# Alternating the taps of two gate groups and moving reciprocals apart on VectorE in a sparse-attention and gated-projection kernel

## The chip, the cores and the metric

The kernel runs on one core of a Trainium2 chip. The core has TensorE (PE in the profile, with its weight loads listed as PEld), VectorE (DVE), ScalarE (ACT), GpSimd (POOL) and a queue that only issues transfers (SP). The metric is the device time of one execution in microseconds; lower is better. The time of the kernel before is the median of three runs.

## The reference

The inputs are q, k and v of 4 batches, 8 heads, 768 positions and 64 dimensions, a table of 3 sampled key blocks for each of 24 blocks of 32 positions, and the weights of a gated projection. All are float32.

```python
scores = q @ k.T / sqrt(64)                      # per batch and head
mask = |blk_i - blk_j| <= 1 or blk_i in (0, 23) or blk_j in (0, 23) or blk_j in sampled_blocks[blk_i]
attn = softmax(where(mask, scores, -1e9))        # the sum gets 1e-9 added before the division
x = (attn @ v), heads side by side               # [4, 768, 512]
gate_pre[t] = sum over k in 0..4 of conv_w[k] * xp[t + k]      # xp: x with 4 zero rows ahead
out = (sigmoid(gate_pre) * (x @ w_val)) @ w_out
```

So each output row needs the attention of its block of queries, a causal convolution of five taps along the sequence for the gate, and two dense 512x512 products.

## The kernel before, in words

**Units and steps.** Query blocks are worked in pairs. A batch has 11 ordinary pairs (each query block sees 8 key blocks) and one global pair (blocks 0 and 23, which see all 24) that is cut into two units. That makes 48 pairs and 52 units. The main loop (line 762) runs one step per unit, and in step n TensorE gets, in this order: the scores of unit n (tiles `sc`, or `s` for a global unit), the weighted values of unit n-2 (`av`), the transposes that bring the finished pair of unit n-3 into channel order (`xp`), the transposes of the weights of unit n-1 (`pt`), and then pieces of the projection (`vp` for x @ w_val, `op` for the product with w_out). The digits of `FILLS` say how many of those pieces a half step gets.

**Order on the engines.** Every engine executes its instructions in the order in which the Python code emits them (`InOrder`, line 77). An instruction that waits holds up all that stand behind it on the same engine.

**A unit on the other engines.** VectorE takes the row maxima of the scores (`mx`, line 457); ScalarE takes the exponentials (`pe`), and after the transposes it copies `pt` to `ptr` (line 475), which the `av` products use as weights. The column of ones in v makes the denominators part of `av`. At the end of a pair `values` (line 479) has VectorE add 1e-9 to the denominators (`rs<-av`), take the reciprocal (`rs<-rs`), and multiply (`x<-av,rs`). There is one `av` buffer (pool `ps_av`, bufs=1), so the next pair's `av` products can't start until `x` has read it. `x` is needed again by the `xp` transposes one step later. All 512 channels sit in four groups of 128 (`CH`), 384 positions at a time, which gives 8 tiles of rows.

**The gate.** `gates` (line 559) is a generator that works one tile of 384 rows. Its accumulators are four slices of `th`. For group f, ScalarE writes tap 0 (`first`, tile form `th<-xT,cw`), VectorE adds taps 1 to 4 (`th<-xT,cw,th`), each on top of the one before, and ScalarE applies a tanh (`th<-th`). The call of `first` for a group and the tanh of a finished one are put behind certain taps. `prepare` (line 721) advances the generators: the digits of `STEPS` say how many times per half step. It first decodes the weights, which arrive as 64-bit numbers, on VectorE and ScalarE (`words`, `wst`, `wv`, `wo`), and only then the gate. After those, it advances `split` (line 589: `xh` on ScalarE and `xl` on VectorE, the two halves of x that `vp` multiplies). `behind` (line 179) delays a call to the start of the next half step while `holding[0]` is set.

Of the kernel before, what the change touches and what calls it, by code (L numbers as in the profile page):

```python
# [12 lines left out]
ALU = mybir.AluOpType  # L13
# [3 lines left out]
B, H, S, D = 4, 8, 768, 64  # L17
# [5 lines left out]
CH = 4  # L23
# [41 lines left out]
def attention_moe(ctx, tc, qb, kb, v, ve, sampled, w_val, conv_w, w_out, ident_in, slot_in, out):  # L65
# [29 lines left out]
    pe, dve, act, pool, sp = (InOrder(e) for e in (nc.tensor, nc.vector, nc.scalar, nc.gpsimd, nc.sync))  # L95
# [83 lines left out]
    def behind(*calls):  # L179

        if holding[0]:
            waiting.extend(calls)
        else:
            for call in calls:
                call()

    def run(calls):
        while calls:
            calls.pop(0)()
# [97 lines left out]
    for bt in batches:  # L287
        order = list(range(NP - 1))
        order.insert(GLOB_AT[bt.b], -1)
        for place, p in enumerate(order):  # L290
            pr = Pair()
# [187 lines left out]
    def values(un):  # L479
        pr = un.pr  # L480
        if un.e == 0:
            pr.av = ps_av.tile([128, 2, 2, DV], F32, tag="av", name="av")
        if pr.glob:
            for h in range(2):
                for c in range(6):
                    pt = un.PT[4 * h + c if c < 4 else 4 + 2 * h + c]
                    for hp in range(HP):
                        cols = slice(BLK * hp, BLK * hp + BLK)
                        hd = 2 * hp + h
                        matmul(  # L490
                            pr.av[cols, un.e, h, :], pt[:, cols], pr.bt.vn[:, c, hd * DV : (hd + 1) * DV],
                            start=c == 0, stop=c == 5, tile_position=(0, BLK * hp),
                        )
        else:
            slots = [(a, h, b, (4 * a + 2 * b + h) * DV) for a in range(2) for h in range(2) for b in range(2)]
            wide = pr.bt.b < WIDE
            if wide:
                for a, h, b, hd in slots:
                    matmul(
                        pr.av[64 * b : 64 * b + 64, a, h, :], un.PT[4 * h + 2 * a][:, 64 * b : 64 * b + 64],  # L500
                        pr.va[:, hd : hd + DV], start=a + h == 0, stop=False, tile_position=(0, 64 * b),
                    )
            for a, h, b, hd in slots:
                for c in range(1 if wide else 0, 2):
                    for j in range(2):
                        rows = slice(64 * b + BLK * j, 64 * b + BLK * j + BLK)
                        vt = pr.vb[:, j, :] if c else pr.va
                        matmul(
                            pr.av[rows, a, h, :], un.PT[4 * h + 2 * a + c][:, rows], vt[:, hd : hd + DV],
                            start=c == 0, stop=a + h == 2 if wide else c == 1, tile_position=(0, rows.start),  # L510
                        )
        if un.last:
            rs = three.tile([128, 2, 2, 2], F32, tag="rs", name="rs")
            dve.tensor_scalar_add(rs[:, 0], pr.av[:, :, :, D], 1e-9)
            dve.reciprocal(rs[:, 1], rs[:, 0])
            pr.x = two.tile([128, 2, 2, D], F32, tag="x", name="x")
            dve.tensor_tensor(
                out=pr.x, in0=pr.av[:, :, :, 0:D], in1=rs[:, 1, :, :, None].to_broadcast([128, 2, 2, D]), op=ALU.mult
            )

    def finish(pr):
# [37 lines left out]
    def gates(m):  # L559

        xT, t, n = m.bt.xT, m.t, m.n
        m.th = two.tile([128, CH, TS], F32, tag="th", name="th")
        acc = [m.th[:, f, 0:n] for f in range(CH)]

        def first(f):
            act.activation(acc[f], xT[:, f, t : t + n], AF.Copy, scale=cw[:, f, 0:1])

        def tanh(f):
            act.activation(acc[f], acc[f], AF.Tanh, scale=0.5)

        first(0)
        yield
        for f in range(CH):
            for k in range(1, KW):
                dve.scalar_tensor_tensor(
                    out=acc[f], in0=xT[:, f, t + k : t + k + n], scalar=cw[:, f, k : k + 1], in1=acc[f],
                    op0=ALU.mult, op1=ALU.add,
                )
                if k == 1 and f + 1 < CH:
                    behind(lambda f=f: first(f + 1))  # L580
                if f and k == 2:
                    behind(lambda f=f: tanh(f - 1))
                yield
        yield
        tanh(CH - 1)
        m.bt.read.add(("gate", m.t))
        yield
# [17 lines left out]
                m.bt.read.add(("split", m.t))  # L605
            yield

    late = []

    def project(m):  # L610

# [76 lines left out]
    def advance(jobs, after=None):  # L688

        m, g = jobs[0]  # L690
        try:
            next(g)
        except StopIteration:
            jobs.pop(0)
            if after is not None:
                after(m)
# [18 lines left out]
    def fill(times=1):  # L715
        for _ in range(times):
            if may_project():
                run(late)
                advance(to_project)

    def prepare(steps):
        for k in range(steps):
            if k == 1:
                run(late)
            if next(decoding, None):
                continue

            if to_gate and (to_gate[0][0].begun or len(gating) < 2):
                to_gate[0][0].begun = True
                gating.add(id(to_gate[0][0]))  # L730
                advance(to_gate, prepared)
        run(late)

        if {CH, CH + 1} <= decoded and len(staged) == 2 * CH and to_split and unread <= {id(to_split[0][0])}:
            advance(to_split, prepared)


    at = {"keys": 0, "values": 0, "copied": 0, "scaled": 0}
# [23 lines left out]
    for n in range(N + LAG_V):  # L762
        step[0] = n

        def more_keys():
            return more("keys", freed(n - 1) + RING, load_keys)

        def more_values():
            return more("values", freed(n - LAG_V - 1) + VRING, load_values)

        if n == 0:
            more_keys()
            numbers_first = {eng: list(block_numbers(pairs[0], eng)) for eng in (POOL, ACT)}
            until("scaled", 0, scale)
            indices(0)
            until("copied", 0, copy_keys)
            more_keys()
            until("copied", 1, copy_keys)
            more_values()
        else:  # L780
            while more_keys() or more_values():
                more_values()
        until("scaled", n + (SCALE_AHEAD if n else 1), scale)
        store()
        k = len(staged)
        if k < 2 * CH and n >= WEIGHTS_AT[k] and (k < 4 or k - 4 in decoded):
            next(weights)

        second_half = []
        if n < N:  # L790
            second_half.append(scores(units[n]))
            if not (n and units[n - LAG_T].pr.glob and units[n - LAG_T].pr.bt.b < HI_MOE):
                run(second_half)
        if n == 0:
            more_keys()
        until("copied", n + COPY_AHEAD, copy_keys)
        if n == 0:
            while more_keys() or more_values():
                more_values()
        if 0 <= n - LAG_V < N:  # L800
            values(units[n - LAG_V])
        if n >= LAG_V:
            while more("values", freed(n - LAG_V) + VRING, load_values):
                pass
        ending = [finish(units[n - LAG_X].pr)] if n >= LAG_X and units[n - LAG_X].last else []
        full = n < N and units[n].pr.glob and units[n].pr.bt.b >= HI_MOE
        for end in ending:
            if not full:
                next(end)

        def end_pairs():
            while ending:
                for _ in ending.pop(0):
                    pass

        if 0 <= n - LAG_T < N:
            pieces = 3 if units[n - LAG_T].pr.glob else 2
            for half, _ in enumerate(transposes(units[n - LAG_T])):
                at_half = 2 * n + min(half, 1)
                run(second_half)  # L820
                run(waiting)
                if half + 1 == pieces:
                    run(copies)
                    end_pairs()
                fill(int(FILLS[at_half]))
                holding[0] = half + 1 < pieces and not may_project()
                prepare(int(STEPS[at_half]))
                holding[0] = False
        else:
            fill(1)  # L830
            prepare(int(STEPS[2 * n]))
        if n == N + LAG_V - 1:
            ending.append(finish(units[N - 1].pr))
        end_pairs()
# [53 lines left out]
```

## Time and profile before

| | |
|---|---|
| Device time, median of 3 runs | 373.05 us (371.3, 373.05, 377.46) |
| Span of the profiled execution | 372.1 us |
| TensorE busy | 349.9 us, 94% of the span |
| VectorE busy | 270.6 us, 73% |
| ScalarE busy | 254.3 us, 68% |
| GpSimd busy | 144.9 us, 39% |
| Taps `th<-xT,cw,th` on VectorE | 128 instructions, 79.2 us |
| `x<-av,rs`, reciprocal, denominators on VectorE | 48 each: 20.4, 8.6 and 7.4 us |

The profiled execution's own time outside the profiler isn't given; its span lies 0.95 us below the median and within the three times. A span is counted from the first to the last instruction. In the rows below a time in front is the start from the beginning of the span, and the second number is a length. A row with xN stands for N instructions that follow one another, and its length runs from the first start to the last end, so that two rows of one engine may overlap by a few hundredths.

### The profile page before, as it was taken

The page shows a single profiled execution, that of the slowest core. Times are in us where ns is not written, and L with a number is a line of the kernel's source. Part 1 is how long each engine was busy: PE and PEld are TensorE (multiplying, and loading weights), DVE is VectorE, ACT ScalarE, POOL GpSimd, SP SyncE. Part 2 cuts the span into 40 slices and gives each one's busy share as a digit, 9 for nine tenths or more (in the row PEclk, how much of TensorE's full clock was granted, in tenths as well). Part 3 has the DMA queues.
Part 4 walks back from the last instruction along what each step waited for, and adds up shares of the span by engine and source line. Part 5 has one row for each costly group of instructions (what it writes and reads, how often), then busy time and mean ns, then how long its engine had stood idle before and what let it go on. Part 6 is the DMA issues. An engine that isn't in the chain of part 4 may idle for free.

```text
span 372.1 us, 15481 instructions
## 1 busy us (share of the span) xinstructions
PE 349.9 (94%) x6274; PEld 276.1 (74%) x6274; DVE 270.6 (73%) x618; ACT 254.3 (68%) x619; POOL 144.9 (39%) x237
## 2 busy tenths in 40 slices
PE   8689998888998999999999999999999999999995
PEld 7456665556666787788779877787888779889894
DVE  4246789888978888678978867577669865979540
ACT  2568689899787857758687587666658766764421
POOL 1856683866573333633352063522531143000000
PEclk9959999999999999999999999999999999999999
DMA  7978886889987365798879367898664373110102
GB/s 229 278 241 277 283 281 226 237 219 299 286 257 248 109 167 146 188 315 232 262 203 289 107 173 214 218 288 250 192 195 130 98 232 99 55 58 28 75 11 85
DMA packets 52582, 72.35 MB, mean 194 GB/s; under 512 B 6944, under 2 KB 34720, under 8 KB 52512
## 3 DMA queue, kind: packets, MB, share of 16 engines
q1 hardware_dynamic: 44896, 47.69, 42.0%
q0 software_dynamic: 7040, 23.43, 22.1%
q8 instruction: 50, 0.82, 0.9%
q10 hardware_dynamic: 576, 0.24, 0.2%
q14 instruction: 20, 0.16, 0.2%
HBM read 65.05 MB, written 6.29 MB: 192 GB/s over the span
## 4 chain that ended last, share of the span: by engine, by line
PE 78%; DVE 8%; ACT 7%; issue 4%; another core or an unknown queue 1%; DMA 1%; ACTq 0%; DVEq 0%
PE vp L83 18%; PE op L83 18%; PE av L83 15%; PE pt L83 11%; PE sc L83 10%; PE xp L83 4%; PE s L83 3%; DVE mx L83 2%; ACT pe L83 2%; ACT ptr L83 2%; DMA sb<-in_sampled 1%; DVE xl L83 1%; DVE wst L83 1%; ACT first L83 1%
## 5 line engine op out<-in xcount | busy, mean ns | idle before, releaser
L83 POOL DMA_INDIRECT vb<-in_v,idx x88 | 87.4, 993 | 158.9 <-PE av L83 129.9
L83 ACT ACTIVATE pe<-sc,mx 128x256 f32<-128x256 f32 x176 | 69.6, 476 | 50.2 <-DVE mx L83 46.3
L83 DVE SCALAR_TENSOR_TENSOR th<-xT,cw,th 128x384 f32<-128x384 f32 x128 | 79.2, 626 | 7.5 <-ACT th L83 5.5
L83 DVE TENSOR_REDUCE mx<-sc 128x2 f32<-128x512 f32 x88 | 56.8, 684 | 38.1 <-PE sc L83 24.6
L83 ACT COPY ptr<-pt 128x512 f32<-128x512 f32 x112 | 64.4, 603 | 9.6 <-PE pt L83 7.1
L83 PE MATMUL sc<-kg,qc 64*32 64x256 f32 x1408 | 54.6, 388 | 6.9 <-DVE cst L83 3.4
L83 POOL COPY kg<-k 128x256 f32<-128x256 f32 (+1 forms) x143 | 56.8, 434 | 9.1 <-DMA k<-in_k 8.0
L83 PE MATMUL op<-wo,yh 128*128 128x512 f32 x192 | 53.6, 401 | 0.0
L83 PE MATMUL vp<-xh,wv 128*128 128x384 f32 x256 | 51.3, 341 | 0.0
L83 PE MATMUL pt<-ident,pe 128*128 128x128 f32 x352 | 50.9, 280 | 0.0
L83 PEld LDWEIGHTS av<-va,ptr 128*32 128x32 f32 (+1 forms) x1056 | 32.2, 119 | 24.9 <-issue 16.4
L83 PE MATMUL av<-va,ptr 128*32 128x65 f32 (+1 forms) x1056 | 42.7, 228 | 4.0 <-issue 3.1
L83 PEld LDWEIGHTS pt<-ident,pe 128*128 128x128 f32 x352 | 42.0, 144 | 3.3 <-DMA qc<-in_q 0.4
L83 PEld LDWEIGHTS vp<-xh,wv 128*128 128x128 f32 x256 | 44.2, 188 | 0.2
L83 PEld LDWEIGHTS sc<-kg,qc 64*32 64x32 f32 x1408 | 24.1, 107 | 26.9 <-issue 16.9
L83 PEld LDWEIGHTS op<-wo,yh 128*128 128x128 f32 x192 | 34.7, 188 | 6.6
L83 PE MATMUL av<-vb,ptr 128*32 128x65 f32 x1408 | 38.3, 224 | 1.3 <-issue 1.3
L83 PEld LDWEIGHTS av<-vb,ptr 128*32 128x32 f32 x1408 | 30.3, 111 | 3.3 <-issue 1.8
L83 PE MATMUL op<-wo,yl 128*128 128x512 f32 x96 | 31.6, 410 | 0.0
L83 ACT CAST yh<-y 128x384 fp32r<-128x384 f32 x32 | 16.6, 519 | 20.4 <-DVE y L83 19.8
L83 DVE SCALAR_TENSOR_TENSOR y<-th,vp 128x384 f32<-128x384 f32 x32 | 17.6, 549 | 13.7 <-PE vp L83 12.3
L83 PE MATMUL vp<-xl,wv 128*128 128x384 f32 x128 | 27.3, 335 | 0.0
(72 smaller groups left out, 441.1 us busy)
## 6 DMA issues: line engine op xcount, KB each, us to landing
kg<-in_k SPq DMA_DIRECT2D x165, 64.0 KB
vn<-in_v SPq DMA_DIRECT2D x12, 520.0 KB
qc<-in_q SPq DMA_DIRECT2D x48, 128.0 KB
k<-in_k SPq DMA_DIRECT2D x12, 512.0 KB
out<-ot SPq DMA_DIRECT2D x23, 256.0 KB
va<-in_v SPq DMA_DIRECT2D x44, 130.0 KB
wst<-in_w_val SPq DMA_DIRECT2D x4, 512.0 KB
wst<-in_w_out SPq DMA_DIRECT2D x4, 512.0 KB
```

The costliest lines, as they stand in the source:

```text
L83: made = getattr(self.eng, name)(*args, **kwargs)
```

## The change

Three things are edited. In `values`, the reciprocal and the product of a finished pair are no longer emitted at once: they go into a list `drip`. A new function `drop` emits from that list, one entry after each advance in `prepare`, one after a step's last transposes, and what is left at the end of the step. In `gates`, `first` is called for two groups at the start and the taps of two groups alternate; the calls of `first` for the other two groups and of the tanhs move accordingly.

```diff
         if un.last:
             rs = three.tile([128, 2, 2, 2], F32, tag="rs", name="rs")
             dve.tensor_scalar_add(rs[:, 0], pr.av[:, :, :, D], 1e-9)
-            dve.reciprocal(rs[:, 1], rs[:, 0])
+            drip.append(lambda: dve.reciprocal(rs[:, 1], rs[:, 0]))
             pr.x = two.tile([128, 2, 2, D], F32, tag="x", name="x")
-            dve.tensor_tensor(
-                out=pr.x, in0=pr.av[:, :, :, 0:D], in1=rs[:, 1, :, :, None].to_broadcast([128, 2, 2, D]), op=ALU.mult
+            drip.append(
+                lambda: dve.tensor_tensor(
+                    out=pr.x, in0=pr.av[:, :, :, 0:D], in1=rs[:, 1, :, :, None].to_broadcast([128, 2, 2, D]), op=ALU.mult
+                )
             )
...
         first(0)
+        first(1)
         yield
-        for f in range(CH):
+        for g in range(0, CH, 2):
             for k in range(1, KW):
-                dve.scalar_tensor_tensor(
-                    out=acc[f], in0=xT[:, f, t + k : t + k + n], scalar=cw[:, f, k : k + 1], in1=acc[f],
-                    op0=ALU.mult, op1=ALU.add,
-                )
-                if k == 1 and f + 1 < CH:
-                    behind(lambda f=f: first(f + 1))
-                if f and k == 2:
-                    behind(lambda f=f: tanh(f - 1))
-                yield
+                for f in (g, g + 1):
+                    dve.scalar_tensor_tensor(
+                        out=acc[f], in0=xT[:, f, t + k : t + k + n], scalar=cw[:, f, k : k + 1], in1=acc[f],
+                        op0=ALU.mult, op1=ALU.add,
+                    )
+                    if g == 0 and k < 3 and f == 1:
+                        behind(lambda k=k: first(k + 1))
+                    if g and k == 1:
+                        behind(lambda f=f: tanh(f - 2))
+                    yield
+        behind(lambda: tanh(CH - 2))
         yield
         tanh(CH - 1)
...
+    def drop(times=2):
+        while drip and times:
+            drip.pop(0)()
+            times -= 1
+
     def prepare(steps):
         for k in range(steps):
             if k == 1:
                 run(late)
             if next(decoding, None):
+                drop(1)
                 continue
 
             if to_gate and (to_gate[0][0].begun or len(gating) < 2):
                 to_gate[0][0].begun = True
                 gating.add(id(to_gate[0][0]))
                 advance(to_gate, prepared)
+                drop(1)
         run(late)
...
                 if half + 1 == pieces:
                     run(copies)
                     end_pairs()
+                    drop(1)
                 fill(int(FILLS[at_half]))
...
+        drop()
         if n == N + LAG_V - 1:
```

What this does to the order of instructions is shown at three places. The first is VectorE at the last pair before the dense products start (122 us in the trace). Before:

```order
L83 TENSOR_REDUCE mx<-sc 128x2 x2
L83 TENSOR_SCALAR rs<-av 128x4
L83 RECIPROCAL rs<-rs 128x4
L83 TENSOR_TENSOR x<-av,rs 128x256
L83 SCALAR_TENSOR_TENSOR th<-xT,cw,th 128x384 x3
```

The same place now:

```order
L83 TENSOR_SCALAR rs<-av 128x4
L83 SCALAR_TENSOR_TENSOR th<-xT,cw,th 128x384
L83 RECIPROCAL rs<-rs 128x4
L83 SCALAR_TENSOR_TENSOR th<-xT,cw,th 128x384
L83 TENSOR_TENSOR x<-av,rs 128x256
L83 SCALAR_TENSOR_TENSOR th<-xT,cw,th 128x384
```

One tap now stands between the denominators and their reciprocal, and another between that and the product. The second place is ScalarE at the start of the first tile's gate (75 us), as a piece of the difference:

```order
 L83 COPY xT<-xp 128x4x64
 L83 CAST wo_152<-words 128x512
-L83 ACTIVATE th<-xT,cw 128x384
+L83 ACTIVATE th<-xT,cw 128x384 x2
 L83 ACTIVATE qc<-qc 128x256
 L83 ACTIVATE pe<-sc,mx 128x256 x4
```

A second `first` stands ahead of the exponentials of that step. The third is ScalarE where the dense products are about to start (119 to 124 us). Before:

```order
L83 CAST wo_152<-words 128x512
L83 ACTIVATE qc<-qc 128x256
L83 ACTIVATE pe<-sc,mx 128x256 x4
L83 COPY ptr<-pt 128x512 x2
```

Now:

```order
L83 CAST wo_152<-words 128x512
L83 ACTIVATE th<-xT,cw 128x384
L83 ACTIVATE qc<-qc 128x256
L83 ACTIVATE pe<-sc,mx 128x256 x4
L83 COPY ptr<-pt 128x512
L83 ACTIVATE th<-xT,cw 128x384
L83 COPY ptr<-pt 128x512
```

Here one `first` comes ahead of the exponentials and another between the two copies to `ptr`. A little earlier (112 us) a second `first` is also put ahead of a `ptr` copy and a cast to `xh`.

## Rows read from the trace of the kernel before

**Rows 1.** The page, part 1: busy time and share of each engine.
```profile
PE 349.9 (94%) x6274; PEld 276.1 (74%) x6274; DVE 270.6 (73%) x618; ACT 254.3 (68%) x619; POOL 144.9 (39%) x237
```

**Rows 2.** Stretches: length; PE, PEld, DVE, ACT, POOL busy; clock; DMA share; GB/s.
```profile
30.00:126.00 96.00, 85.00 (x2021) 60.07 (x2022) 81.41 (x179) 81.50 (x212) 56.94 (x101) 1.00 0.82 249
126.00:345.00 219.00, 217.99 (x3905) 179.50 (x3904) 169.26 (x377) 151.08 (x352) 71.98 (x98) 1.00 0.62 180
```

**Rows 3.** Waits of PE from 126 to 345: total, times, longest.
```profile
PE av L83 <- issue: 0.8, 2, 0.4
```

**Rows 4.** Timeline of DVE: start, length, instruction, count.
```profile
227.38 1.26 DVE L83 SCALAR_TENSOR_TENSOR th<-xT,cw,th 128x384 f32<-128x384 f32 x2
228.56 0.49 DVE L83 TENSOR_SCALAR qc<-qc 128x256 f32<-128x256 f32 x1
...
237.44 0.15 DVE L83 TENSOR_SCALAR rs<-av 128x4 f32<-128x4 f32 x1
237.63 0.18 DVE L83 RECIPROCAL rs<-rs 128x4 f32<-128x4 f32 x1
237.84 0.42 DVE L83 TENSOR_TENSOR x<-av,rs 128x256 f32<-128x256 f32 x1
238.19 0.61 DVE L83 SCALAR_TENSOR_TENSOR th<-xT,cw,th 128x384 f32<-128x384 f32 x1
...
254.74 0.61 DVE L83 SCALAR_TENSOR_TENSOR th<-xT,cw,th 128x384 f32<-128x384 f32 x1
255.27 0.55 DVE L83 TENSOR_TENSOR xl<-xT,xh 128x384 fp32r<-128x384 f32 x1
```

**Rows 5.** The chain that ended last, in order of time, 48 to 78: start, length.
```profile
51.00 0.42 DVE x L83
...
62.31 0.42 DVE x L83
...
64.80 0.55 DVE mx L83
...
65.37 0.62 ACT pe L83 x2
...
76.43 1.19 PE sc L83 x30
```

**Rows 6.** Timeline of ACT from 74 to 76.
```profile
74.74 0.61 ACT L83 ACTIVATE th<-xT,cw 128x384 f32<-128x384 f32 x1
75.25 0.40 ACT L83 ACTIVATE qc<-qc 128x256 f32<-128x256 f32 x1
75.56 1.55 ACT L83 ACTIVATE pe<-sc,mx 128x256 f32<-128x256 f32 x4
```

**Rows 7.** Timeline of ACT and DVE at 112 to 114.
```profile
112.64 0.57 ACT L83 CAST xh<-xT 128x384 fp32r<-128x384 f32 x1
113.57 1.33 DVE L83 TENSOR_TENSOR xl<-xT,xh 128x384 fp32r<-128x384 f32 x1
```

**Rows 8.** Timeline of DVE, ACT and PE from 121 to 124.
```profile
121.92 0.15 DVE L83 TENSOR_SCALAR rs<-av 128x4 f32<-128x4 f32 x1
122.31 0.42 DVE L83 TENSOR_TENSOR x<-av,rs 128x256 f32<-128x256 f32 x1
122.66 1.79 DVE L83 SCALAR_TENSOR_TENSOR th<-xT,cw,th 128x384 f32<-128x384 f32 x3
122.88 1.09 ACT L83 COPY ptr<-pt 128x512 f32<-128x512 f32 x2
123.53 0.34 PE L83 MATMUL av<-va,ptr 128*64 128x65 f32 x4
124.02 0.57 PE L83 MATMUL av<-va,ptr 128*64 128x65 f32 x12 [0.15 <-ACT ptr L83]
```

**Rows 9.** Timeline of DVE and PE from 276 to 281.
```profile
278.06 2.78 DVE L83 SCALAR_TENSOR_TENSOR th<-xT,cw,th 128x384 f32<-128x384 f32 x3
280.19 1.00 PE L83 MATMUL av<-vn,ptr 128*32 128x65 f32 x56
```

More of the change, by code (lines that the diff above doesn't have):

```diff
@@ L606, in split @@
             yield
-    late = []
+    late, drip = [], []
     def project(m):
@@ L824, in attention_moe @@
                     end_pairs()
+                    drop(1)
                 fill(int(FILLS[at_half]))
```

## The prediction

> **What bounds the kernel now.** I read the page's first part, then the table of stretches, then the waits of TensorE, then the chain of waits, and the timeline last. The page says that TensorE is busy 94% of the span and VectorE 73% [rows 1]; that is an average over two very different stages, so the reader should go on to the stretches at once. From 126 to 345 us TensorE is busy 217.99 of 219.00 us [rows 2], and its longest kind of wait there sums to 0.8 us and is for nothing on VectorE [rows 3]. In that stage VectorE could be infinitely fast and the end would move by about 1 us. From 30 to 126 us TensorE is busy 85.00 of 96.00 us, so 11.0 us are idle, while VectorE and ScalarE are busy some 81 us each [rows 2]. Only there can an edit on VectorE buy time. The chain of waits says how much: in this stage it runs over VectorE in a few places, such as x at 51.00 and at 62.31, the latter followed by the row maxima and the exponentials [rows 5]. After 345 us the tail is dense products, to which this change adds and from which it takes nothing.
>
> **What the edits are worth on VectorE.** Taps first. Two taps that follow each other on the same group take 1.18 us from the first start to the start of what stands behind them (227.38 to 228.56), and a tap that is followed by something independent takes 0.53 (254.74 to 255.27) [rows 4]. So a dependent tap costs 0.65, and alternating saves 0.12 for each pair of neighbours on one group. The order before holds 55 such pairs, 10 of them ahead of 126 us: 6.6 us in all, 1.2 us where it may count.
>
> Reciprocal and product next. From the denominators to what follows x takes 0.75 us (237.44 to 238.19): 0.19 to the reciprocal, 0.21 to x, 0.35 to the next [rows 4]. The overlap of independent neighbours is 0.08 (0.61 less 0.53), so set apart the three cost 0.07, 0.10 and 0.35, that is 0.52, and 0.23 is saved. The new order sets all three apart for 30 of the 48 pairs. For 13 the product stands right behind the reciprocal, which leaves 0.12 of saving, and for 5 nothing moves. That is 6.9 + 1.6 = 8.5 us in all. Between 39 and 126 us there are 8 of the first kind and 7 of the second: 2.7 us. With the taps, VectorE is spared 15.1 us over the kernel, and 3.9 us where TensorE has gaps.
>
> A rule speaks against both savings. The Trainium skill, page "VectorE: DVE Perf Modes", section "The DRAIN you can't avoid", says that the next operation can't start until the pipe of the one before has emptied, and that a chain with and without semaphores took the same time. By that rule the two terms are nothing, and the sum below would be 0.5 us more. The trace here disagrees: 0.53 against 0.65 us [rows 4].
>
> **What of it reaches the end.** Of the 3.9 us I count only what lies on the chain: the two products of rows 5, at 0.23 each, **-0.5 us**. In the rest of the early stage VectorE either waits for scores or stands behind ScalarE, so it is earlier for nothing; the cover is TensorE's own work and ScalarE's exponentials and copies, and if that cover were gone the 3.9 would count in full. No tap of the early stage is on the chain with a dependent neighbour. Behind 126 us the 11.2 us that are left are hidden by TensorE [rows 2].
>
> **What it costs on ScalarE.** `first` for the second group is now issued with the first one, and other calls move with it. Three of the places lie where TensorE waits for ScalarE.
> - At 74.74 a second `first` goes ahead of the exponentials that start at 75.56 with no gap before them [rows 6]. The second half of the next scores starts at 76.43 [rows 5], when exponentials have freed its buffer. One `first` takes 0.51 us from start to start (74.74 to the scaling of the queries at 75.25): **+0.5 us**, or nothing if later gaps absorb it.
> - At 112 one more `first` stands ahead of a cast to xh that now ends at 113.21; 0.5 later it ends at 113.7, and the subtraction that started at 113.57 [rows 7] waits for it: **+0.2 us**, as row maxima follow.
> - At 123 one `first` now stands between the two copies to ptr. The twelve products at 124.02 waited for the second copy [rows 8], and dense work begins right behind: **+0.5 us**.
> Where such calls went away they were covered, since exponentials waited for row maxima.
>
> **What the later x costs.** x is the last reader of the only av buffer, and TensorE's next av products stand in order behind it, with all of TensorE's later work. So its new end is what matters. The tightest pair is that of rows 8. There denominators start at 121.92; now a tap, the reciprocal, a tap and x follow: 0.07 + 0.53 + 0.10 + 0.53 + 0.42, so x ends at 123.57 and av started at 123.53. That is a loss of 0.04 us, **0.0**. The inserted operations run earlier than before, because x no longer stands ahead of them; that is why the delay is so small. Later on, the tightest pair has two of three taps end by 279.91 even if nothing moves forward, x 0.34 later at 280.25, and av started at 280.19 [rows 9]. With what is moved forward there is room. SP's and GpSimd's queues keep their order.
>
> The sum against the profiled execution: 372.1 - 0.5 + 0.5 + 0.2 + 0.5 + 0.0 = 372.8 us. The profiled span lies 0.95 us under the median of 373.05, and one of three runs is 4.4 above it, so a median may land between 372.8 and 373.75; I take **373.2 us**.
>
> **Rivals.**
> - *VectorE is on the chain nearly everywhere before 126 us.* For it: VectorE and ScalarE are as busy as TensorE there, and 11.0 us are idle [rows 2]. Against it: rows 5 leave much of the chain to TensorE and ScalarE. All 3.9 us would count, and the ScalarE delays be absorbed: 372.1 - 3.9 = 368.2 us. Chance 0.17, between 368.2 and 371.
> - *The product comes too late, and the av products wait for it (slower).* Place: the single av buffer in the steps before 124 us. It decides as soon as the inserted operations don't run earlier than before, because they wait for ScalarE or are stretched. In rows 8 the second tap then ends at 122.66 + 1.19 = 123.85 and x at 124.19, 0.66 us late. Eighteen pairs end up to there; with half of that loss in half of them, 9 x 0.33 = 3.0 us, so 372.8 + 3.0 = 375.8 us; with it in all of them 5.9 us, 378.7. For it: before, av started only 0.80 us after x ended (122.73 to 123.53) [rows 8], less than two taps. Against it: the working above. Chance 0.16.
> - *It doesn't do what it says.* Five products are not moved and 13 are moved together with their reciprocal, and the rows of the taps might not shorten. Then only ScalarE's delays stay: 372.1 + 1.2 = 373.3 us, chance 0.05, which the time alone can't tell from the forecast.
>
> **How the numbers follow.** The forecast has a chance of 0.54 (371 to 375), and 0.08 is left for what I haven't seen. The range of 8 in 10 reaches from part of the first rival to most of the second: 369.3 to 377.0 us. A measurement of this kernel tells about 2% from no change, 7.5 us, so 365.6 and 380.5 are the limits. The first rival in full stays inside, and so does the second; beyond them is only what I haven't seen: 0.04 for faster, 0.04 for slower, 0.92 within.
>
> **What would show it.** Right: VectorE's rows of taps run at 0.53 us apart, and its busy time falls by some 10 us (0.08 for each 0.12 saved, the rest being gaps), while TensorE's busy time and the stretch from 126 to 345 stay; the av products at 124 wait for the second copy to ptr; the av products of rows 8 start within 1.5 us of 124.02. Wrong: they start over 2 us earlier (first rival), or over 2 us later with av products waiting for x on the way (second). If the end moves and they don't, my claim that TensorE covers all behind them is wrong.

## The result, and the profile after

The changed kernel took 376.47 us, median of six runs (374.78 to 380.2); the kernel before took 374.27 us beside it (371.3 to 429.07, six runs). The ratio is **1.0131, 95% interval [1.0083, 1.0179]**; a ratio compares, of each kernel, only the executions near its shortest time, while medians and lists of times hold them all. I had forecast no change. The profiled execution of the changed kernel has a span of 376.4 us and took 378.2, so a time lies 1.8 us above its span here.

First the page and the stretches, as in [rows 1, 2].

```profile
PE 351.1 (93%) x6274; PEld 277.3 (74%) x6274; DVE 259.4 (69%) x618; ACT 253.4 (67%) x619; POOL 145.1 (39%) x237
```

```profile
30.00:126.00 96.00, 84.50 (x1976) 59.73 (x1977) 76.13 (x174) 80.11 (x208) 55.46 (x96) 0.98 0.78 239
126.00:345.00 219.00, 215.02 (x3882) 176.44 (x3881) 157.18 (x369) 147.11 (x344) 71.30 (x98) 0.99 0.61 180
```

VectorE is spared 11.2 us (270.6 to 259.4). Yet TensorE has lost 3 us of work in the stretch that was full: 215.02 where it was 217.99. Its two largest waits there (total, times, longest; in [rows 3] the largest summed to 0.8 us):

```profile
PE vp L83 <- ACT ot L83: 3.4, 1, 3.4
PE av L83 <- issue: 0.3, 1, 0.3
```

The 3.4 us are one wait, and its engine is one that the prediction never named. The timeline around it, SP (called SyncE below), ACT and PE (the bracket is the idle time before a row and what ended it; "..." marks rows left out):

```profile
265.08 3.79 SPq L83 DMA_DIRECT2D kg<-in_k  x6
268.96 0.38 SPq L83 DMA_DIRECT2D out<-ot  x1
...
272.88 0.60 ACT L83 ACTIVATE ot<-op 128x512 f32<-128x512 f32 x1 [4.97 <-DMA out<-ot]
...
269.24 0.85 PE L83 MATMUL vp<-xl,wv 128*128 128x384 f32 x4
273.53 2.58 PE L83 MATMUL vp<-xh,wv 128*128 128x384 f32 x8 [3.44 <-ACT ot L83]
275.91 1.48 PE L83 MATMUL vp<-xl,wv 128*128 128x384 f32 x4
```

Read it from the end. The products `vp` need a buffer of results that ScalarE empties into `ot` (the eviction). `ot` has two buffers, and the older one can be written again only when its store to `out` has landed. That store was issued by SyncE at 268.96, behind six key loads, and landed 3.8 us later. The same place in the trace of the kernel before:

```profile
262.80 3.87 SPq L83 DMA_DIRECT2D kg<-in_k  x6
266.77 0.38 SPq L83 DMA_DIRECT2D out<-ot  x1
...
269.14 0.60 ACT L83 ACTIVATE ot<-op 128x512 f32<-128x512 f32 x1 [0.47 <-DMA out<-ot]
...
270.68 1.56 PE L83 MATMUL vp<-xh,wv 128*128 128x384 f32 x8
```

ScalarE waited for the same store there too, 0.47 us, and TensorE did not feel it. In the changed kernel 4.97 us on ScalarE became 3.44 on TensorE, so TensorE had 1.5 us in hand. Of the 4.50 us that ScalarE waits longer, 2.19 come from the later issue (266.77 and 268.96), 1.55 from a slower landing (2.37 and 3.92 us from the issue to the eviction's start), and 0.76 from ScalarE being ready earlier (268.67 and 267.91). The wait has a second price (length; PE, PEld, DVE, ACT, POOL busy; granted clock; DMA share; GB/s):

```profile
270.00:272.00 2.00, 0.09 (x1) 0.00 (x0) 0.55 (x1) 0.00 (x0) 0.00 (x0) 1.00 0.91 285
272.00:274.00 2.00, 0.47 (x3) 0.47 (x4) 0.00 (x0) 1.12 (x3) 0.00 (x0) 0.99 0.39 127
274.00:276.00 2.00, 2.00 (x8) 2.00 (x7) 0.82 (x2) 1.65 (x4) 0.00 (x0) 0.50 0.39 110
276.00:278.00 2.00, 2.00 (x29) 1.33 (x35) 0.00 (x0) 0.00 (x0) 0.00 (x0) 0.65 0.72 220
```

Behind the idle 3.4 us the granted clock is 0.50, that is 1.2 GHz, and the twelve products take 3.86 us where twelve take 2.09 elsewhere: 1.8 us more. Comparing the start of each step's `av` products in the two traces gives the sum. At the step at 131.5 us the two executions differ by -0.03 us (131.56 and 131.53). At the step at 243 us the changed kernel is 0.75 us ahead (243.40 and 242.65). Near 235 us TensorE pauses, with no cause that the profile shows, twice in the kernel before, 0.8 us in all [rows 3], and once in the changed one, 0.3 us. At one place near 270 us the difference jumps by 5.2 us, which is 3.4 + 1.8, to 4.45, and at the end 4.3 are left.

The -0.03 us is itself a balance of two things that the prediction didn't have. In the kernel before, the profiled execution reaches the step at 33.5 us 2.5 us later than the changed one. The changed one then loses these 2.5 us again, most of it here:

```profile
58.20 0.62 PE L83 MATMUL sc<-kg,qc 64*32 64x256 f32 x4 [2.07 <-issue]
```

Before, this pause was 0.44 us. Behind it the granted clock falls to 0.50 as well, from 59 to 62 us. In the other profiles with the whole change in this stage the same pause is 1.3 to 2.2 us, in those with neither edit there 0.2 to 0.9; the moved product alone gives 1.0 and 1.6 (e2, e11). `pt`, a little earlier, waits some 0.8 us less for ScalarE in return, so the step takes 6.9 to 7.3 us with the change where the clock stays, and 6.7 to 7.3 without. Only this profile and e12's lose the clock there.

Last, the chain of waits of the changed kernel ahead of that place (start, length, what):

```profile
244.79 7.92 DMA vn<-in_v
...
256.30 6.65 DMA vn<-in_v
...
263.61 1.27 SPq L302
...
268.96 3.81 DMA out<-ot
272.88 0.61 ACT ot L83
273.53 3.86 PE vp L83 x12
```

It leaves TensorE altogether: store, SyncE's issues, and ahead of these the landings of two value loads. In the trace of before the chain from 200 to 272 us holds no transfer.

### The profile page after: what moved, and what is told of

It is laid out like the page before. It is cut to its first block, busy times and chain, and to the rows that moved or that the text cites. A ratio compares the mean times of both kernels' runs of the same rounds, so it can differ in the third digit from the quotient of the medians.

```text
span 376.4 us, 15486 instructions
## 1 busy us (share of the span) xinstructions
PE 351.1 (93%) x6274; PEld 277.3 (74%) x6274; DVE 259.4 (69%) x618; ACT 253.4 (67%) x619; POOL 145.1 (39%) x237
## 4 chain that ended last, share of the span: by engine, by line
PE 70%; ACT 8%; DMA 7%; DVE 5%; issue 5%; SPq 4%; ACTq 1%; POOL 0%; POOLq 0%; DVEq 0%
PE vp L83 15%; PE op L83 15%; PE av L83 14%; PE sc L83 10%; PE pt L83 10%; DMA vn<-in_v 4%; SPq L83 3%; PE xp L83 3%; PE s L83 2%; ACT pe L83 2%; DMA k<-in_k 2%; DVE mx L83 2%; ACT ptr L83 2%; DMA out<-ot 1%; ACT first L83 1%
## 5 line engine op out<-in xcount | busy, mean ns | idle before, releaser
L83 POOL DMA_INDIRECT vb<-in_v,idx x88 | 90.4, 1028 | 165.7 <-PE av L83 138.8
L83 POOL COPY kg<-k 128x256 f32<-128x256 f32 (+1 forms) x143 | 54.0, 417 | 9.5 <-DVE tmp L83 5.9
L83 PE MATMUL vp<-xh,wv 128*128 128x384 f32 x256 | 52.3, 346 | 3.4 <-ACT ot L83 3.4
```

The source lines that it names most:

```text
L83: made = getattr(self.eng, name)(*args, **kwargs)
```

## The experiments

Theories. **O**: the loss is the eviction's wait for an output store near 270 us. **S**: it is the first calls of a gate, at worse places on ScalarE. **P**: it is the later product. The experiments came in four groups (e1 to e4, e5 to e8, e9 to e12, e13 to e16), each with its own runs of the kernel before, and ratios are to these; their medians went from 368.96 to 371.53 us, so times of different groups are not compared. Each experiment has one trace.

**e1_taps and e2_drip: each kind of edit alone.**

```diff
-            drip.append(lambda: dve.reciprocal(rs[:, 1], rs[:, 0]))
+            dve.reciprocal(rs[:, 1], rs[:, 0])
```

That is e1 against the changed kernel (the product goes the same way); e2 keeps `drip` and has `gates` as it was before.

> Taps alternate as in the change, but the reciprocal and the product stand right behind the denominators as before. If the loss comes with the new places of ScalarE's first calls (theory S, the ScalarE term of the prediction): ratio to the kernel before 1.005 to 1.015, as the whole change. If it comes from the later product (theory P): 0.995 to 1.002. If it is a wait for output stores near 270 us that depends on how the transfers fall (theory O): anything from 1.00 to 1.015, with that wait in the profile when it is slow.

> Reciprocal and product spread out as in the change, taps and ScalarE's calls as before. Theory S: 0.995 to 1.002. Theory P: 1.005 to 1.015, with TensorE's av products later by the time that x is late. Theory O: as in the run with the taps alone, the profile decides.

Measured: 1.0011 [0.9952, 1.0070] and 1.0037 [0.9989, 1.0084]. Neither shows a loss clear of its interval, though e2's reaches 0.8%. ScalarE waited for the store 3.08 us in e1 and 2.77 in e2, and in e1 TensorE also waited 1.6 us for VectorE (`vp` for `y`), as it does in e16:

```profile
263.18 0.60 ACT L83 ACTIVATE ot<-op 128x512 f32<-128x512 f32 x1 [3.08 <-DMA out<-ot]
```

**e3_after_ot3 and e4_before_ot3: a third output buffer**, in the changed kernel and in the one before. No instruction moves. (To make room, the edit also shrinks a table `sv` that this kernel doesn't use, and the weights' `words`, which share the buffers of `ot`, get the third one too.)

```diff
-            ot = two.tile([128, DM], F32, tag="ot", name="ot")
+            ot = three.tile([128, DM], F32, tag="ot", name="ot")
```

> The changed kernel with three output buffers instead of two, so that an eviction needn't wait for the last but one store. The order of instructions is unchanged. Theory O: the wait of 3.4 us of TensorE near 270 us is gone, ratio to the kernel before 0.995 to 1.003. Theories S and P: the ratio stays at 1.01 to 1.015.

> The kernel before with three output buffers. If the kernel before has the same wait for stores in part of its runs, it gains too: ratio 0.99 to 0.998 and a narrower spread of times. If only the change brings the wait: 0.998 to 1.002.

Measured: 0.9943 [0.9897, 0.9989] and 0.9957 [0.9911, 1.0002]. The two are level, so S and P don't account for a per cent. The weights' third buffer is no rival that shows: the step that came at 131.5 us above comes at 123.35 and 122.69 here, and at 122.52 and 124.25 in e1 and e2 with two buffers. And all that TensorE still waits for in e3 between 126 and 345 us is this:

```profile
PE pt L83 <- ACT ptr L83: 0.2, 1, 0.2
```

**e5_after, e6_after_store_first, e7_before_store_late, e8_before.** e5 is the changed kernel once more and e8 the kernel before. The other two move one store and nothing else.

```diff
 e6 (changed kernel):
         else:
+            store()
             while more_keys() or more_values():
 ...
-        store()
 e7 (kernel before):
+        if n not in (42,):
             store()
```

> The changed kernel itself, once more, to see whether its loss repeats in the company of the other experiments. Theory O (the loss is a ScalarE eviction near 270 us that waits for an output store, which SyncE issues behind six key loads): the wait of TensorE's vp on ACT ot shows again with 2 to 4 us at one place between 126 and 345 us, and the ratio to before is 1.006 to 1.015, above the 1.001 and 1.004 of the two halves of the change. Theory S (the first calls of a gate on ScalarE come at worse places, all before 126 us): 1.003 to 1.004, with or without the wait. Theory C (the two first profiles differ by chance of an execution and the loss of 1.3% does not repeat): a ratio whose interval holds 1.000, with a wait for the store of about 1 us as in both halves.

> The changed kernel with one move: in each step of the main loop SyncE issues the waiting output stores ahead of the step's loads of queries, keys and values, where it issued them behind. Still two output buffers. Theory O: the store near 269 us is issued about 5 us earlier, the eviction no longer waits, the wait of vp on ACT ot falls to under 0.3 us, and the ratio to before is 0.993 to 0.998, as with three output buffers (0.994). Theory S and theory P (the later product of the denominators): nothing changes against the changed kernel itself, 1.004 to 1.013. Against it: SyncE may now wait for an eviction while the loads queue behind it; then waits of sc or av on DMA kg or vb appear and the gain is eaten.

> The kernel before, with none of the change, but with the one output store that it issues at 266.8 us held back by one step, so that it is issued behind six more key loads, near 274.5 us. It doubles the suspected cost by itself. Theory O: the eviction that waited 0.5 us in the kernel before waits some 8 us (0.5 plus the 7.7 of the later issue), TensorE's vp waits 5 to 7 us for ACT ot at that one place, and the ratio to before is 1.012 to 1.020. If the rows of the output stores did not matter to TensorE (my prediction's claim that behind 126 us no other queue matters): 1.000, with no such row.

> The kernel before itself, one look, for its profile on the chip of the experiments. Theory O: the eviction near 263 to 270 us already waits for the store by 0.5 to 3 us, since the kernel before with three output buffers was 0.4% shorter than with two; TensorE's vp then waits 0 to 1.6 us for ACT ot. Without O: no such row, and the 0.4% of the third buffer would be chance.

Measured: e5 1.0103 [1.0057, 1.0149], so the loss repeats. e7 **1.0177 [1.0112, 1.0241]**: one store held back in the kernel before, and issued together with the next one, costs at least as much as the whole change.

```profile
268.72 0.84 SPq L83 DMA_DIRECT2D out<-ot  x2
...
270.99 0.60 ACT L83 ACTIVATE ot<-op 128x512 f32<-128x512 f32 x1 [6.70 <-DMA out<-ot]
```

ScalarE waits 6.70 us and TensorE 5.2: the same 1.5 us in hand. In e8 it is 2.81 and 1.3, in e5 4.71 and 3.2. What e5 doesn't pay is the clock:

```profile
268.00:270.00 2.00, 0.31 (x2) 0.32 (x3) 0.00 (x0) 0.96 (x2) 0.00 (x0) 1.00 0.53 162
270.00:272.00 2.00, 2.00 (x14) 1.75 (x13) 0.82 (x2) 1.80 (x5) 0.00 (x0) 1.00 0.36 105
```

After 3.2 idle us the granted clock stayed at 1.00 in that execution, so only the wait was paid. e6 missed its 0.993 to 0.998: 1.0072 [1.0035, 1.0109]. The wait for the store is gone, as expected, but SyncE now waits for evictions while loads stand behind it, the risk I had named. Its waits from 126 to 262 us:

```profile
SPq L83 <- ACT ot L83: 5.8, 2, 4.4
```

Against e8 its `av` products lose 1.7 us between the steps at 161 and 248 us of e8. They were 1.8 us late by 127 us already; one trace each can't tell whether that is the edit or the execution.

**e9_early and e10_late: the change up to 126 us alone, and from there on alone.**

```diff
+            if not CHANGED(step[0] < EARLY):
+                run(drip)
...
+        if CHANGED(m.bt.b == 0):
```

`EARLY` is 22, and `CHANGED` is the condition itself in e9 and its opposite in e10; where it doesn't hold, `values` emits both operations at once and `gates` is as before.

> The change made only in the first part of the run: the taps of the first batch alternate, and the reciprocal and product of the units handled before the 22nd step (about 126 us) wait behind other VectorE operations; from there on the order is word for word that of the kernel before. Theory O (the loss is the wait for the output store near 270 us and comes from what the change does to the queues after 126 us): the eviction waits for the store as long as in the kernel before on the same chip (vp waits 0 to 1.6 us for ACT ot), ratio 1.001 to 1.004, the rest being the 1.2 us of ScalarE terms that I had priced at 75, 112 and 123 us. Theory S (first calls of a gate, all before 126 us): 1.003 to 1.005 and nothing left for the other half. If the early shift sets the later lag by chance: 1.008 to 1.013 with a wait of 3 us.

> The other half in time: the order of the kernel before up to the 22nd step (the first batch's taps and the first units' products), the changed order from there on. Theory O: vp waits 2.5 to 4 us for ACT ot near 270 us, as in the changed kernel, and the ratio to before is 1.004 to 1.011. Theory S: 0.998 to 1.001, with the wait of the kernel before.

Measured: 1.0002 [0.9964, 1.0041] and 1.0006 [0.9966, 1.0046]. I had expected one half to carry the loss. By the ratios neither does, and in both profiles the eviction doesn't wait at all; for e10:

```profile
261.65 0.38 SPq L86 DMA_DIRECT2D out<-ot  x1
...
264.64 0.62 ACT L86 ACTIVATE ot<-op 128x512 f32<-128x512 f32 x1
```

Both profiles are of shorter executions, though (370.46 and 369.86 us). Of the twelve times of e9 four lie above 374 us, of those of e10 five, and of the kernel before beside them 3 of 29. No trace of such an execution was kept, so whether they met the wait isn't shown. What the two traces do show is that neither half brings the wait in every execution. It depends on how late SyncE comes to that store, and on how long the store then takes to land, as the table below and the text behind it show.

**e11_drip_ot3 and e12_after_act_store: two attempts at a better kernel.** e11 is e2 with three output buffers. e12 is the changed kernel with

```diff
-            stores.append((out[m.bt.b, m.t + r * 128 : m.t + r * 128 + 128, :], ot))
+            act.dma_start(out[m.bt.b, m.t + r * 128 : m.t + r * 128 + 128, :], ot)
```

> A version meant to beat both kernels: the reciprocal and product of the denominators spread out, the taps and the gates as in the kernel before, and three output buffers. Theory O: no wait of vp for ACT ot; without the ScalarE terms of the alternating taps it is 0 to 1.5 us below the changed kernel with three buffers, so the ratio to before is 0.990 to 0.996. If the third buffer's 0.5% was chance: 0.998 to 1.004.

> The changed kernel, two output buffers, but each output store is issued by ScalarE right behind the eviction that fills it, and none by SyncE except the last. SyncE runs without a pause from about 214 to 270 us in the profiles, so a store that it doesn't issue frees 0.4 to 2 us of it. Theory O: a store is in flight within 1 us of its eviction, the wait of vp on ACT ot is gone, and the ratio to before is 0.990 to 0.998. Against it: ScalarE loses some 0.4 us at each of the 23 stores; where TensorE waits for ptr from ScalarE (two places after 126 us) that shows, up to 1 us in all. Theory S and P: as the changed kernel, 1.007 to 1.013.

Measured: e11 0.9989 [0.9958, 1.0020], no gain; e12 **1.0282** [1.0213, 1.0351], the worst of all. ScalarE stood still for 6 us between an eviction and the issue of its store, until an earlier value load had landed, and TensorE waits for ScalarE in new places, the longest 3.1 us (`pt` for `rest`):

```profile
260.56 0.62 ACT L83 ACTIVATE ot<-op 128x512 f32<-128x512 f32 x1
266.93 0.34 ACTq L83 DMA_DIRECT2D out<-ot  x1
267.31 0.51 ACT L83 CAST xh<-xT 128x384 fp32r<-128x384 f32 x1 [6.13 <-DMA va<-in_v]
```

My price for a store on ScalarE, 0.4 us, was the length of the issue and left out what the issue waits for.

**e13 to e16: the third buffer beside the changed kernel, and a late SyncE by itself.** e13 is the changed kernel, e14 and e15 are e3 and e4 again. e16 is the kernel before with seven small loads more on SyncE, into tiles that nobody reads:

```diff
+        if n == 37:
+            for e in extra:
+                sp.dma_start(e, slot_in[0:1, 0:8])
         store()
```

> The changed kernel again, for a comparison with the next two beside the same runs of the kernel before. Theory O: 1.007 to 1.014, with a wait of vp for ACT ot of 2.5 to 4 us near 270 us. If the loss came and went with the chip or the hour: 0.998 to 1.004.

> The changed kernel with three output buffers, again. Theory O: no wait of vp for ACT ot, and 0.994 to 1.002 of the kernel before, that is 1.0 to 1.5% below the changed kernel of the same call. If something else than the store makes the loss: within 0.4% of the changed kernel.

> The kernel before with three output buffers, again. Theory O: no wait, 0.995 to 1.000 of the kernel before, and the same as the changed kernel with three buffers within 0.4% (the 1.2 us of ScalarE terms against it are 0.3%).

> The kernel before, no instruction of VectorE, ScalarE or TensorE moved; SyncE issues seven more transfers of 32 bytes, that nobody reads, in the step whose loads it issues near 222 to 226 us. At 0.33 to 0.5 us an issue that makes SyncE, which has no pause there, some 2.5 to 3 us later up to 270 us, as late as in the changed kernel. Theory O with a late SyncE as its cause: the store near 262 to 267 us is issued 2 to 3 us later against TensorE's products, vp waits 2.5 to 4.5 us for ACT ot, ratio 1.006 to 1.013. If SyncE makes the time up before 270 us, or if the lateness of the store isn't what counts: a wait of 0 to 1.6 us and 1.000 to 1.003.

Measured: e13 1.0042 [0.9986, 1.0098], e14 0.9985 [0.9943, 1.0026], e15 1.0021 [0.9977, 1.0064], e16 **1.0177** [1.0096, 1.0258]. By its ratio the loss isn't clear in e13; by its median it is there: e13 took 375.04 us, e14 370.31 and e15 370.74, beside 371.53 for before. The twelve times of e13 fall into two groups: three are 369.81 to 370.60, the other nine 374.15 to 377.81. With the third buffer ten of twelve (e14) and eight of twelve (e15) are under 372, the others 373.35 to 375.69. So long executions have another source too, which no trace shows, and in e13 they are the rule. The profile of e13 is one of the nine (a wait of 3.5 us, then a clock of 0.53); that the other eight met the same wait is likely and not shown.

In e16 nothing of VectorE or ScalarE was moved. Its timeline, and TensorE's longest waits from 126 to 345 us:

```profile
226.35 2.10 SPq L83 DMA_DIRECT2D extra<-in_slot  x7
...
269.06 0.13 SPq L83 DMA_DIRECT2D out<-ot  x1
...
274.25 0.60 ACT L83 ACTIVATE ot<-op 128x512 f32<-128x512 f32 x1 [5.74 <-DMA out<-ot]
```

```profile
PE vp L83 <- ACT ot L83: 4.4, 2, 4.2
PE vp L83 <- DVE y L83: 1.6, 1, 1.6
```

A SyncE that is made some 4 us late is enough for the wait, with a store that took 5.2 us from issue to eviction. The ratio is above the 1.006 to 1.013 that I expected; 1.6 us of another wait came with it, and the clock fell to 0.50.

## How late SyncE is

SyncE's queries are a clock for its lateness. In every profile it issues one load of queries 1.73 to 1.76 us after the start of a certain step's `av` products (near 214 us); the store in question comes just ahead of the eighth load after it. From the one load to the other, in the kernels whose stores stand where they stood:

```profile
214.45 1.19 SPq L83 DMA_DIRECT2D qc<-in_q  x1
267.80 0.54 SPq L83 DMA_DIRECT2D qc<-in_q  x1
```

that is 53.35 us for the kernel before, and for the changed one 55.57:

```profile
214.43 1.26 SPq L83 DMA_DIRECT2D qc<-in_q  x1
270.00 0.54 SPq L83 DMA_DIRECT2D qc<-in_q  x1
```

| Order of the instructions | the eight loads, us | ScalarE / TensorE waited, us |
|---|---|---|
| before (first profile, e8) | 53.35, 53.90 | 0.47 / 0, 2.81 / 1.3 |
| before, 3 buffers (e4, e15) | 52.23, 52.55 | none |
| before, SyncE busy (e16) | 57.53 | 5.74 / 4.2 |
| changed (first profile, e5, e13) | 55.57, 55.80, 56.17 | 4.97 / 3.4, 4.71 / 3.2, 5.02 / 3.5 |
| changed, 3 buffers (e3, e14) | 53.40, 56.50 | none |
| taps (e1), product (e2) | 54.59, 53.34 | 3.08 / 1.5, 2.77 / 1.2 |
| product, 3 buffers (e11) | 54.41 | none |
| early (e9), late (e10) | 52.80, 51.61 | none |

The full change makes SyncE 2 to 3 us late in four of five profiles; no half of it does so by as much. e14 is the test of the theory: its SyncE is as late as in any profile of the changed kernel, and with a third buffer it costs nothing. Lateness isn't all of it: e2's SyncE is as punctual as that of the first profile before (53.34 and 53.35), yet ScalarE waits 2.77 us where it waited 0.47. From issue to eviction the store took 2.4 us in that first profile, 4.2 in e1, e2 and e8, and 3.3 to 3.9 in the changed kernel with two buffers. What stays **open** is why SyncE is late under the changed order. The chain of the changed kernel shows the kind of thing: SyncE waits for transfers that take 6.65 and 7.92 us to land. That it is settled by how the queues happen to stand to each other is my guess, not shown. It isn't settled by the order alone: e3 has the changed order and a punctual SyncE, and e10, whose order behind 126 us is that of the change, has the most punctual of the table (51.61).

## Why the prediction was wrong

- *VectorE's savings.* Right. Busy time fell by 11.2 us where some 10 were expected. At the place of [rows 8] the operations now start at the distances that I summed:

```profile
121.39 0.15 DVE L83 TENSOR_SCALAR rs<-av 128x4 f32<-128x4 f32 x1
121.46 0.61 DVE L83 SCALAR_TENSOR_TENSOR th<-xT,cw,th 128x384 f32<-128x384 f32 x1
121.99 0.17 DVE L83 RECIPROCAL rs<-rs 128x4 f32<-128x4 f32 x1
122.07 0.59 DVE L83 SCALAR_TENSOR_TENSOR th<-xT,cw,th 128x384 f32<-128x384 f32 x1
122.58 0.42 DVE L83 TENSOR_TENSOR x<-av,rs 128x256 f32<-128x256 f32 x1
```

  0.07, 0.53, 0.08 and 0.51, against 0.07, 0.53, 0.10 and 0.53. By the rule that the prediction took from the Trainium skill, page "VectorE: DVE Perf Modes", section "The DRAIN you can't avoid", there would have been nothing to gain; the trace disagrees with it, as before. The prediction left out that the same section also says that a next operation that is not held back starts earlier; with that the trace agrees: the reciprocal and the product here start 0.08 us before the tap ahead of them ends.
- *The later x.* Right in the main: `av` products wait for x at one place in the changed kernel, that of [rows 9], where the prediction saw room:

```profile
284.70 0.60 PEld L83 LDWEIGHTS av<-vn,ptr 128*32 128x32 f32 x39 [0.48 <-DVE x L83]
```

  A weight load waits 0.48 us, and the step's products slip by 0.07. The rival by which the late product holds up `av` before 124 us is refuted, and so is the one by which VectorE is on the chain nearly everywhere.
- *ScalarE's costs of 0.5, 0.2 and 0.5 us, and the -0.5 for x.* Not shown in sum. The twelve products at 124 start at 124.00 and wait 0.57 us for the second copy, as forecast. Between the two kernels with three buffers (e4, e3) the `av` starts slip by 0.40 us behind the first place, by nothing near the second, and by 0.39 behind the third. But other steps of this pair slip by up to 1.5 us either way, and over the whole stage, up to the step at 131.5 us, it loses 0.7 us, e5 against e8 1.2, and e14 against e15 gains 1.2. The net +0.7 of the prediction is within what executions differ by.
- *The step that failed*: "Behind 126 us the 11.2 us that are left are hidden by TensorE", and with it "SP's and GpSimd's queues keep their order". The first is true of VectorE's time and was taken as true of everything. The second is true, and it says nothing of *when* a queue comes to its instructions. In their place the runs showed a SyncE that is 2 to 3 us late at one output store, and an eviction that waits 4.97 us for it, 3.4 of them on TensorE, with 1.8 us of slower clock behind. A third buffer takes that away (e3, e14), and one late store (e7) or a late SyncE (e16) brings it without the change. I had read the waits of TensorE only [rows 3], where a wait that the slack of 1.5 us absorbs doesn't appear. ScalarE's row at 269.14, with its 0.47 us for a store, was in the same trace and said that this place was 1 us from the brink. The prediction did name the sign: the end moved and the early `av` products didn't.
- *The time.* The sum of 372.8 us was a span, and it came to 376.4. The term that I didn't have is 5.2 us (3.4 of wait, 1.8 of slower clock). Against it stand the +0.7 of mine that didn't appear in this pair, 0.75 us that TensorE gained near 235, and 0.2 in the tail. I also took 0.95 us between span and time, and it is 1.8. That 376.47 us still lies within my range of 369.3 to 377.0 is luck: its upper part came from the rival of the late product, which is not what happened.

Of all versions only e3 lay below the kernel before by more than its interval (0.9943 [0.9897, 0.9989]), and e14, the same kernel again, did not (0.9985). A third output buffer brings the changed kernel level with the kernel before or a little under it, and does the same for the kernel before itself, so what gain there is belongs to the buffer and not to the change.

## What to carry to other kernels

Before saying that an engine covers the rest, list the waits of the *other* engines and queues in that stretch, and look for those which end just in time: they are the ones that a harmless reordering can turn into a stall. A queue that issues one transfer after another without a pause is a resource like an engine, and a store that stands in it behind loads can need one buffer more, as here (e3, e14). Where a kernel's single times fall into two groups, ask which wait some executions meet and others don't, before pricing instructions.

## What the runs showed of the hardware

- A stall of TensorE can cost more than its length. After idle stretches of 3.4, 3.5, 4.2 and 5.2 us (changed kernel, e13, e16, e7) the granted clock fell to 0.50 to 0.53 (about 1.2 GHz) within the next 4 us, and after 2.1 and 2.2 us near 58 us in two profiles (changed kernel, e12). After 1.3 us (e8), 2.7 (e2, near 107 us), 3.1 (e12, near 191 us) and 3.2 us (e5) it stayed at 1.00. So the length of the stall alone didn't decide.
- The same output store of 256 KB landed some 2.4 us after its issue in one profile of the kernel before (266.77 to 269.14) and 4.1 us in the other (e8). A value load of 520 KB took 6.65 and 7.92 us in the chain above.
- How long one issue holds SyncE varies: a load of queries took 0.54 us at 267.80 in the kernel before, 1.19 at 214.45 and 2.37 at 226.92. The seven small loads of e16 took 0.3 us each.
